# Moving GpSimd's elementwise work of the feed-forward part and the attention to VectorE and ScalarE

## The chip, the cores and the metric

One Trainium2 chip, one core of it. The core has TensorE (PE, matmuls; its weight loads are shown as PEld), VectorE (DVE), ScalarE (ACT), GpSimd (POOL) and SyncE (SP, which issues the transfers here). The metric is the device time of one execution in microseconds (us), the median of several runs.

## The reference

Three parts behind one another, in float32 (weights come as 64-bit numbers): attention with a window and a few always visible keys, a feed-forward part with a norm in front, and a part that turns the channels by an angle, mixes over tokens and ends in a gated channel product.

```python
batch, n_heads, seq, head_dim = (2, 8, 768, 64)      # d_model = 512
n_sink, window = (4, 128)
scores = np.where(is_sink | in_window, scale * q @ k.T, -1e9)
a = softmax(scores) @ v
# feed-forward
xn = (x - mu) / np.sqrt(var + 1e-06) * g_ln
x = x + np.maximum(xn @ w_ch1, 0.0) @ w_ch2            # 512 -> 2048 -> 512
# mixing
theta = x @ w_theta
yr = np.einsum('ts,bsd->btd', w_tok_r, x * np.cos(theta))
yi = np.einsum('ts,bsd->btd', w_tok_i, x * np.sin(theta))
u = x + yr + yi
return u + np.maximum(u @ w_ch, 0.0)
```

## The kernel before

The 1536 tokens are cut into six pieces of 256 tokens (two tiles of 128). For each piece the attention is computed head by head (8 heads), then the norm (`norm`), then the feed-forward part. The hidden width of 2048 is cut into 16 blocks; a *unit* `u` multiplies one block of both weight matrices: `first(u)` gives the hidden block `h`, `second(u)` adds its product to the accumulators. Two pieces run in the units at a time, and each pair of pieces joins eight units after the other, so there are 56 units. The order of TensorE's instructions is written out by hand (attention steps are put between the matmuls of the units by `advance`); that of the other engines is made by a scheduler that plays the program against its own model of durations. Each engine works off its queue in order. After the units comes the mixing part (`gate`, `mix`, `final`).

Precision: a float32 number is split into a high part, which TensorE takes as `fp32r`, and a low part, the difference; a product is then three matmuls (high x high, high x low, low x high). The high part is a copy on ScalarE, the low part a subtraction on another engine. The splits are these: `split_qk` (L234, queries and keys), `split_v` (L202 or L204 and L205, values, in float16), `split_w12` (L609 and L610, the feed-forward weights, once in each `first` and `second` from unit 8 on; `wh` and `wl` have three buffers each), L646 (the hidden block, whose input lies in PSUM), `split_w` (L684 and L685, weights of the mixing part).

The weights come as 64-bit numbers. `load64` makes float32 of them in four steps: L517 (VectorE) takes the sign, L518 (ScalarE) rescales the exponent word in place, L521 (GpSimd) or L524 (ScalarE) takes the last bits, L525 (VectorE) puts the words together. The 32 tiles of the feed-forward weights go by L521, those of the mixing part by L524. Four staging tiles take the transfers of the feed-forward weights; the next transfer into one is issued when L525 has freed it.

GpSimd's part of the work before: L610 up to unit 50 (VectorE does those of the last five units), L234 but for the first, L204 and L205 but for the first four tiles, L521, L629 (the low half of the first piece's normalized tokens), L574 (the norm's factor `gain` for pieces 2 to 5), L563 (a power), and in the mixing part L685 and L738.

Of the kernel before, what the change touches and what calls it, by code (L numbers as in the profile page):

```python
# [8 lines left out]
F32 = mybir.dt.float32  # L9
# [5 lines left out]
AF = mybir.ActivationFunctionType  # L15
# [56 lines left out]
class Net:  # L72
# [110 lines left out]
    def split_v(self, b, t):  # L183

        if (b, t) in self.v3:
            return
        nc, p = self.nc, self.att
        r = p["vr"].tile([128, DM], F32, tag="vr", name="vr")
        nc.sync.dma_start(out=r, in_=self.vt[b, t])
        eng = nc.vector if len(self.v3) < V_DVE else nc.gpsimd  # L190
        if t == NT:
            o = p["v"].tile([128, DM], F16, tag="vk", name="vk", bufs=1)
            nc.scalar.activation(o, r, AF.Copy, scale=VSC)
            r, lo, hi = r[64:96], o[64:96], o[64:96]
            self.v3[b, t] = o
        else:
            o = p["v"].tile([128, 2, DM], F16, tag="v", name="v")
            hi, lo = o[:, 0], o[:, 1]
            nc.scalar.activation(hi, r, AF.Copy, scale=VSC)
            self.v3[b, t] = hi, lo  # L200
        if eng is nc.vector:
            eng.scalar_tensor_tensor(out=lo, in0=r, scalar=VSC, in1=hi, op0=ALU.mult, op1=ALU.subtract)  # L202
        else:
            eng.tensor_scalar(out=r, in0=r, scalar1=VSC, scalar2=0.0, op0=ALU.mult, op1=ALU.add)  # L204
            eng.tensor_tensor(out=lo, in0=r, in1=hi, op=ALU.subtract)  # L205

    def range_v(self, b, t):

# [296 lines left out]
            yield  # L505


    def load64(self, src, stage, dst, tag, eng=None):

        nc = self.nc  # L510
        n = dst.shape[-1]
        raw = stage.tile([128, n, 2], I32, tag=tag, name="raw")
        nc.sync.dma_start(out=raw.rearrange("p n w -> p (n w)"), in_=src.bitcast(I32))
        hi, flat = raw[:, :, 1], raw.rearrange("p n w -> p (n w)")
        half = flat.bitcast(U16).rearrange("p (n w) -> p n w", w=4)
        parts = dst.bitcast(U16).rearrange("p (n w) -> p n w", w=2)
        nc.vector.tensor_scalar(out=parts[:, :, 1], in0=half[:, :, 3], scalar1=0x8000, scalar2=None, op0=ALU.bitwise_and)  # L517
        nc.scalar.activation(hi.bitcast(F32), hi.bitcast(F32), AF.Copy, scale=2.0 ** -112)  # L518

        if eng:  # L520
            eng.tensor_scalar(out=parts[:, :, 0], in0=half[:, :, 1], scalar1=2.0 ** -13, scalar2=2.0 ** -14 - 0.5,  # L521
                              op0=ALU.mult, op1=ALU.add)
        else:
            nc.scalar.activation(parts[:, :, 0], half[:, :, 1], AF.Copy, scale=2.0 ** -13, bias=2.0 ** -14 - 0.5)  # L524
        nc.vector.scalar_tensor_tensor(out=dst, in0=hi, scalar=3, in1=dst, op0=ALU.logical_shift_left,  # L525
                                       op1=ALU.bitwise_or)

# [7 lines left out]
    def load_w12(self, f):  # L535
        if f in self.w12f:
            return
        self.w12f[f] = []
        for e in range(2):
            t = self.wraw.tile([128, DM], I32, tag="w", name="w12")  # L540
            self.rawp.append(self.rawp.pop(0))
            self.load64(self.w12[f, e], self.rawp[-1][0], t, self.rawp[-1][1], self.nc.gpsimd)
            self.w12f[f].append(t.bitcast(F32))

    def stats(self, piece, half):
# [7 lines left out]
    def norm(self, piece):  # L553

        nc = self.nc
        mv = self.ln.tile([128, PIECE, 2], F32, tag="mv", name="mv")
        rs = self.ln.tile([128, PIECE], F32, tag="rs", name="rs")
        x, bn = self.x[piece], self.bn.pop(piece)
        xn = [self.ln.tile([128, DM], F32, tag="xn", name="xn", bufs=2) for _ in range(PIECE)]
        for i in range(PIECE):  # L560
            nc.vector.bn_aggr(out=mv[:, i], in_=bn[:, i])
        nc.scalar.activation(rs, mv[:, :, 1], AF.Copy, bias=1e-6)
        nc.gpsimd.tensor_tensor(out=rs, in0=rs, in1=self.mhalf, op=ALU.pow)  # L563
        if piece < DIRECT:
            for i, a in enumerate(xn):
                nc.vector.scalar_tensor_tensor(out=a, in0=x[:, i], scalar=mv[:, i, 0:1], in1=self.gain,
                                               op0=ALU.subtract, op1=ALU.mult)
            for i, a in enumerate(xn):
                nc.vector.tensor_scalar(out=a, in0=a, scalar1=rs[:, i:i + 1], scalar2=None, op0=ALU.mult)
        else:  # L570
            for i, a in enumerate(xn):
                nc.vector.tensor_scalar(out=a, in0=x[:, i], scalar1=mv[:, i, 0:1], scalar2=rs[:, i:i + 1],
                                        op0=ALU.subtract, op1=ALU.mult)
                nc.gpsimd.tensor_tensor(out=a, in0=a, in1=self.gain, op=ALU.mult)  # L574
        self.xnorm[piece] = xn

    def norm_T(self, piece):
# [23 lines left out]

        return piece % 2 if len(active(u)) > 1 else 0

    def split_w12(self, f, e, u=0):
        nc = self.nc
        r = self.w12f[f][e]
        hi = self.wsp.tile([128, DM], F32R, tag="wh", name="wh")
        lo = self.wsp.tile([128, DM], F32R, tag="wl", name="wl")
        nc.scalar.activation(hi, r, AF.Copy)  # L609
        (nc.vector if u >= UNITS - 5 else nc.gpsimd).tensor_tensor(out=lo, in0=r, in1=hi.bitcast(F32), op=ALU.subtract)  # L610
        return hi, lo

    def first(self, u):

        nc, part = self.nc, active(u)
        if u < WHOLE:
            h = self.hp.tile([128, PC], F32, tag="hh", name="hh")
            ps = self.ps_h.tile([128, 512], F32, tag="h", name="h")
            self.h[u] = h
            for k in range(KD):  # L620
                nc.tensor.matmul(ps[:, 0:PC], self.w12f[u][0][:, k * 128:(k + 1) * 128], self.x32[:, k],
                                 start=k == 0, stop=k == KD - 1)
            nc.scalar.activation(h, ps[:, 0:PC], AF.Relu)
            yield
            if u == WHOLE - 1:
                hi, lo = (x[:, :, 0] for x in self.xn)
                for k in range(KD):
                    nc.scalar.activation(hi[:, k], self.x32[:, k], AF.Copy)
                    nc.gpsimd.tensor_tensor(out=lo[:, k], in0=self.x32[:, k], in1=hi[:, k].bitcast(F32), op=ALU.subtract)  # L629
            return  # L630
        wh, wl = self.split_w12(u % NF, 0, u)
# [18 lines left out]
    def second(self, u):  # L650
# [2 lines left out]
        if u < WHOLE:  # L653
            prods = [(self.h.pop(u), self.w12f[u][1])]
        else:
            wh, wl = self.split_w12(u % NF, 1, u)
            hh, hl = self.h.pop(u)
            prods = [(hh, wh), (hh, wl), (hl, wh)]
        for piece in active(u):
# [131 lines left out]
    def run(self, general):  # L791
# [276 lines left out]
```

## Time and profile before

| | us |
|---|---|
| median of 3 runs | 630.4 |
| lowest and highest run | 625.32, 630.4 |
| profiled execution | 629.58 |
| its span, first to last instruction | 627.8 |

| engine | busy us | share of the span | instructions |
|---|---|---|---|
| PE | 570.5 | 91% | 3545 |
| DVE | 385.2 | 61% | 813 |
| ACT | 334.1 | 53% | 738 |
| POOL | 275.5 | 44% | 228 |

An instruction is told by its line and engine, by `output<-input` in the program's names and by its operands (partitions x elements, type); `x32` is their number. "Idle before" is the time the engine stood still in front of such instructions, with what ended it. A wait is written as `who <- for whom: total us, times, longest us`. In a table of stretches each engine has its busy us and, in brackets, its instructions; PEclk is the granted clock of TensorE as a share of 2.4 GHz.

### The profile page before, as it was taken

How to read it: one execution, taken by the hardware profiler on the slowest of the kernel's cores; microseconds unless marked ns; L12 is line 12 of the kernel's file. 1: busy time of each engine (PE TensorE's matmuls, PEld its weight loads, DVE VectorE, ACT ScalarE, POOL GpSimd, SP SyncE). 2: the span in 40 equal slices, each digit the busy share in tenths (PEclk: the TensorE clock that was granted, in tenths of full speed). 3: DMA queues.
4: the chain of work that ended last, by engine and by line, in shares of the span. 5: the costliest groups of instructions: out<-in, count | busy, mean ns of one | idle time of the engine just before them, and what ended most of it. 6: DMA issues, size and time to landing. Idle time of an engine off the chain costs nothing.

```text
span 627.8 us, 9676 instructions
## 1 busy us (share of the span) xinstructions
PE 570.5 (91%) x3545; PEld 470.6 (75%) x3545; DVE 385.2 (61%) x813; ACT 334.1 (53%) x738; POOL 275.5 (44%) x228
## 2 busy tenths in 40 slices
PE   4864779699999999999999969999999889999996
PEld 3753556466777776777788758888899789999996
DVE  5699999666455666737454331126898879754262
ACT  5674767376655655665545533346676666632120
POOL 4376684234673665556357634450334432201100
PEclk9999998799999999999999979999999999999998
DMA  6357756344503343232412220000323312011102
GB/s 255 116 197 250 251 197 206 77 105 83 119 18 80 82 98 65 65 64 45 69 60 93 99 78 0 2 0 1 101 70 119 115 66 69 1 34 34 36 27 81
DMA packets 54794, 55.39 MB, mean 88 GB/s; under 512 B 40016, under 2 KB 43088, under 8 KB 54736
## 3 DMA queue, kind: packets, MB, share of 16 engines
q1 hardware_dynamic: 54736, 54.67, 29.7%
q8 instruction: 30, 0.49, 0.3%
q14 instruction: 28, 0.23, 0.1%
HBM read 42.08 MB, written 3.15 MB: 72 GB/s over the span
## 4 chain that ended last, share of the span: by engine, by line
PE 53%; DVE 20%; ACT 7%; DMA 5%; issue 4%; POOL 3%; ACTq 0%; POOLq 0%; DVEq 0%; SPq 0%
PE acc L667 17%; PE h L641 16%; PE m L752 5%; PE f L783 5%; PE s L259 5%; DVE st L525 2%; DMA raw<-w 2%; DMA raw<-wtok 2%; DVE w L525 2%; PE pv L439 2%; PE th L711 2%; DVE w L517 2%; DVE st L517 1%; ACT raw L518 1%; ACT st L524 1%
## 5 line engine op out<-in xcount | busy, mean ns | idle before, releaser
L610 POOL TENSOR_TENSOR wl<-w,wh 128x512 fp32r<-128x512 f32 x86 | 113.6, 1323 | 116.7 <-ACT wh L609 87.5
L641 PE MATMUL h<-xT,wh 128*128 128x512 f32 (+1 forms) x384 | 94.7, 382 | 0.0
L609 ACT ACTIVATE wh<-w 128x512 fp32r<-128x512 f32 x96 | 60.1, 628 | 60.3 <-PE acc L667 39.0
L361 ACT ACTIVATE p<-p,st 128x272 f32<-128x272 f32 (+1 forms) x96 | 47.7, 497 | 59.4 <-DVE st L358 59.4
L641 PEld LDWEIGHTS h<-xT,wh 128*128 128x128 f32 x384 | 66.3, 188 | 15.4 <-issue 1.2
L667 PE MATMUL acc<-wh,hh 128*128 128x512 f32 x176 | 73.6, 418 | 0.0
L667 PE MATMUL acc<-wl,hh 128*128 128x512 f32 x176 | 69.7, 396 | 0.5 <-POOL wl L610 0.5
L667 PE MATMUL acc<-wh,hl 128*128 128x512 f32 x176 | 69.6, 395 | 0.0
L646 DVE SCALAR_TENSOR_TENSOR hl<-h,hh 128x512 fp32r<-128x512 f32 (+1 forms) x48 | 30.8, 641 | 52.8 <-ACT hh L645 52.8
L358 DVE CUSTOM_DVE_ANT_0 p<-s,mask 128x272 f32<-128x272 f32 (+1 forms) x96 | 39.0, 409 | 32.3 <-PE s L259 31.5
L518 ACT ACTIVATE raw<-raw 128x512 f32<-128x512 f32 (+1 forms) x52 | 37.8, 727 | 25.2 <-DVE w L517 16.3
L234 POOL TENSOR_TENSOR lo<-raw,hi 128x672 fp32r<-128x672 f32 (+1 forms) x23 | 36.9, 1604 | 31.8 <-ACT hi L233 31.6
L738 POOL TENSOR_TENSOR x<-xh,xl 128x512 f32<-128x512 f32 x12 | 19.3, 1609 | 67.7 <-DVE r L732 67.7
L641 PE MATMUL h<-xT,wl 128*128 128x512 f32 (+1 forms) x192 | 48.0, 372 | 0.0
L259 PE MATMUL s<-hi 64*128 64x272 f32 (+1 forms) x96 | 38.7, 409 | 10.2 <-ACT hi L233 6.9
L439 PEld LDWEIGHTS <-wt 128*128 128x128 f16 x576 | 23.4, 103 | 26.7 <-issue 12.3
L259 PEld LDWEIGHTS s<-hi 64*128 64x128 f32 x96 | 20.0, 212 | 27.9 <-issue 10.4
L439 PE MATMUL pv<-v,wt 128*128 128x64 f16 x528 | 27.7, 201 | 14.4 <-DVE x L456 8.3
L667 PEld LDWEIGHTS acc<-wh,hh 128*128 128x128 f32 x176 | 33.6, 191 | 9.3 <-issue 0.8
L385 DVE SCALAR_TENSOR_TENSOR w<-p,w 128x512 f16<-128x512 f32 (+2 forms) x40 | 35.2, 879 | 7.9 <-ACT w L384 7.5
L641 PEld LDWEIGHTS h<-xT,wl 128*128 128x128 f32 x192 | 34.4, 188 | 6.5
L667 PEld LDWEIGHTS acc<-wh,hl 128*128 128x128 f32 x176 | 33.5, 190 | 7.8 <-DVE hl L646 0.3
(290 smaller groups left out, 1544.6 us busy)
## 6 DMA issues: line engine op xcount, KB each, us to landing
raw<-w SPq DMA_DIRECT2D x32, 512.0 KB, 4.3
raw<-wtok SPq DMA_DIRECT2D x12, 768.0 KB, 4.2
raw<-qk SPq DMA_DIRECT2D x16, 336.0 KB, 3.1
vr<-vt SPq DMA_DIRECT2D x14, 256.0 KB, 3.0
out_dram<-o SPq DMA_DIRECT2D x24, 128.0 KB, 1.7
raw<-qk SPq DMA_DIRECT2D x8, 272.0 KB, 3.8
raw<-wth SPq DMA_DIRECT2D x4, 512.0 KB, 3.3
raw<-wch SPq DMA_DIRECT2D x4, 512.0 KB, 3.3
```

What stands on the lines that cost most here:

```text
L234: eng.tensor_tensor(out=lo, in0=r, in1=hi.bitcast(F32), op=ALU.subtract)
L259: self.nc.tensor.matmul(ps, q[:, c], k[:, k0:k0 + kn], start=j == 0, stop=j == 2)
L358: self.newest = [nc.vector.tensor_tensor_reduce(out=e, in0=ps[:, c0:WIN], in1=self.mask[min(t, 2)], scale=-0.125, scalar=3e38, op0=ALU.add ...
L361: nc.scalar.activation(e, e, AF.Exp, bias=st[:, 0, i:i + 1], scale=-1.0, accum_out=st[:, 1, i:i + 1])]
L385: nc.vector.scalar_tensor_tensor(out=o[1], in0=src, scalar=PSC, in1=o[0], op0=ALU.mult, op1=ALU.subtract)
L439: nc.tensor.matmul(pv[:, i * D:(i + 1) * D], a, m, start=j == 0, stop=j == len(prods) - 1)
L518: nc.scalar.activation(hi.bitcast(F32), hi.bitcast(F32), AF.Copy, scale=2.0 ** -112)
L609: nc.scalar.activation(hi, r, AF.Copy)
L610: (nc.vector if u >= UNITS - 5 else nc.gpsimd).tensor_tensor(out=lo, in0=r, in1=hi.bitcast(F32), op=ALU.subtract)
L641: nc.tensor.matmul(ps[:, 0:n], a[:, k * 128:(k + 1) * 128], x[:, k, c], start=m == 0, stop=m == 11)
L667: nc.tensor.matmul(ps, a[:, c], w, start=m == 0 and n == 0, stop=m == NF - 1 and n == len(prods) - 1)
L752: nc.tensor.matmul(ps, z[i][e][:, c * 128:(c + 1) * 128], w[:, t], start=s == 0 and m == 0 and c % 2 == 0, stop=s == NT - 1 and m == 5 and ...
```

## The change

Elementwise work of GpSimd goes to VectorE: the low parts of queries and keys (L234), of values (L204 and L205, two instructions, become the one of L202), of the feed-forward weights (L610) and of the first piece's tokens (L629). For pieces 2 to 5 the norm takes the form that pieces 0 and 1 have, two instructions of VectorE for each tile. The last bits of the feed-forward weights (L521) go to ScalarE, by the instruction of L524. On GpSimd stay the power of the norm (L563), the low parts of the mixing part's weights (L685) and the sum of L738, beside what is done once at the start.

```diff
@@ split_v
-        eng = nc.vector if len(self.v3) < V_DVE else nc.gpsimd
...
-        if eng is nc.vector:
-            eng.scalar_tensor_tensor(out=lo, in0=r, scalar=VSC, in1=hi, op0=ALU.mult, op1=ALU.subtract)
-        else:
-            eng.tensor_scalar(out=r, in0=r, scalar1=VSC, scalar2=0.0, op0=ALU.mult, op1=ALU.add)
-            eng.tensor_tensor(out=lo, in0=r, in1=hi, op=ALU.subtract)
+        nc.vector.scalar_tensor_tensor(out=lo, in0=r, scalar=VSC, in1=hi, op0=ALU.mult, op1=ALU.subtract)
@@ load64 (load_w12 no longer passes nc.gpsimd as eng)
-        if eng:
-            eng.tensor_scalar(out=parts[:, :, 0], in0=half[:, :, 1], scalar1=2.0 ** -13, scalar2=2.0 ** -14 - 0.5,
-                              op0=ALU.mult, op1=ALU.add)
-        else:
-            nc.scalar.activation(parts[:, :, 0], half[:, :, 1], AF.Copy, scale=2.0 ** -13, bias=2.0 ** -14 - 0.5)
+        nc.scalar.activation(parts[:, :, 0], half[:, :, 1], AF.Copy, scale=2.0 ** -13, bias=2.0 ** -14 - 0.5)
@@ norm
-        if piece < DIRECT:
...
-        else:
-            for i, a in enumerate(xn):
-                nc.vector.tensor_scalar(out=a, in0=x[:, i], scalar1=mv[:, i, 0:1], scalar2=rs[:, i:i + 1],
-                                        op0=ALU.subtract, op1=ALU.mult)
-                nc.gpsimd.tensor_tensor(out=a, in0=a, in1=self.gain, op=ALU.mult)
+        for i, a in enumerate(xn):
+            nc.vector.scalar_tensor_tensor(out=a, in0=x[:, i], scalar=mv[:, i, 0:1], in1=self.gain,
+                                           op0=ALU.subtract, op1=ALU.mult)
+        for i, a in enumerate(xn):
+            nc.vector.tensor_scalar(out=a, in0=a, scalar1=rs[:, i:i + 1], scalar2=None, op0=ALU.mult)
@@ split_w12
-        (nc.vector if u >= UNITS - 5 else nc.gpsimd).tensor_tensor(out=lo, in0=r, in1=hi.bitcast(F32), op=ALU.subtract)
+        nc.vector.tensor_tensor(out=lo, in0=r, in1=hi.bitcast(F32), op=ALU.subtract)
@@ first
-                    nc.gpsimd.tensor_tensor(out=lo[:, k], in0=self.x32[:, k], in1=hi[:, k].bitcast(F32), op=ALU.subtract)
+                    nc.vector.tensor_tensor(out=lo[:, k], in0=self.x32[:, k], in1=hi[:, k].bitcast(F32), op=ALU.subtract)
@@ run (the engine that attn_fast hands to split_qk)
-        side = attn(nc.gpsimd)
+        side = attn(nc.vector)
```

## Rows read from the trace of the kernel before

**Rows 1.** the profile page: span and number of instructions

```profile
span 627.8 us, 9676 instructions
```

**Rows 2.** Busy us by stretch (instructions); then granted clock, DMA share, GB/s

```profile
core 0: us, PE busy (x) PEld busy (x) DVE busy (x) ACT busy (x) POOL busy (x), PEclk, DMA share, GB/s
30.00:120.00 90.00, 64.24 (x358) 45.05 (x358) 84.25 (x176) 58.62 (x150) 57.02 (x53) 0.92 0.64 207
120.00:330.00 210.00, 205.29 (x1242) 153.69 (x1243) 124.13 (x329) 122.87 (x323) 111.65 (x88) 1.00 0.33 72
360.00:390.00 30.00, 25.10 (x104) 20.37 (x103) 6.98 (x10) 10.72 (x17) 13.14 (x10) 0.89 0.13 50
450.00:540.00 90.00, 85.74 (x621) 80.19 (x620) 77.18 (x101) 59.43 (x91) 33.76 (x20) 1.00 0.25 85
```

**Rows 3.** TensorE's waits, 30 to 125 us: total us, times, longest

```profile
PE tp L587 <- DVE xn L569: 10.8, 3, 8.2
PE pv L439 <- DVE x L456: 8.3, 3, 3.7
```

**Rows 4.** Timeline of VectorE: start us, us, instruction, [idle before <-releaser]

```profile
73.16 0.67 DVE L525 SCALAR_TENSOR_TENSOR w<-raw,w 128x512 int32<-128x512 int32 x1
73.75 0.45 DVE L517 TENSOR_SCALAR w<-raw 128x512 uint16<-128x512 uint16 x1
...
82.81 1.41 DVE L525 SCALAR_TENSOR_TENSOR w<-raw,w 128x512 int32<-128x512 int32 x1
84.14 1.02 DVE L517 TENSOR_SCALAR w<-raw 128x512 uint16<-128x512 uint16 x1
...
130.32 0.18 DVE L391 SCALAR_TENSOR_TENSOR w<-p,w 128x32 f16<-128x32 f32 x1
```

**Rows 5.** Timeline of GpSimd at the same places

```profile
74.28 1.13 POOL L521 TENSOR_SCALAR w<-raw 128x512 uint16<-128x512 uint16 x1 [0.99 <-DMA raw<-w]
...
82.39 1.28 POOL L610 TENSOR_TENSOR wl<-w,wh 128x512 fp32r<-128x512 f32 x1
83.75 2.04 POOL L521 TENSOR_SCALAR w<-raw 128x512 uint16<-128x512 uint16 x2
```

**Rows 6.** Groups by line, VectorE, 30 to 120 us: busy us, mean ns | idle before

```profile
L525 DVE SCALAR_TENSOR_TENSOR w<-raw,w 128x512 int32<-128x512 int32 x32 | 28.4, 894 | 0.8 <-POOL w L521 0.7
L517 DVE TENSOR_SCALAR w<-raw 128x512 uint16<-128x512 uint16 x32 | 28.3, 890 | 2.3 <-DMA raw<-w 2.3
```

**Rows 7.** Groups by line, GpSimd, 30 to 120 us

```profile
L521 POOL TENSOR_SCALAR w<-raw 128x512 uint16<-128x512 uint16 x31 | 29.2, 943 | 21.1 <-DMA raw<-w 19.9
L234 POOL TENSOR_TENSOR lo<-raw,hi 128x672 fp32r<-128x672 f32 x6 | 10.5, 1754 | 3.5 <-ACT hi L233 3.2
L205 POOL TENSOR_TENSOR v<-vr,v 128x512 f16<-128x512 f32 x3 | 4.1, 1360 | 0.2
```

**Rows 8.** Timeline of ScalarE at 341 us

```profile
340.87 0.80 ACT L524 ACTIVATE st<-raw 128x512 uint16<-128x512 uint16 x1 [1.78 <-DMA raw<-wth]
341.54 0.64 ACT L518 ACTIVATE raw<-raw 128x512 f32<-128x512 f32 x1
```

**Rows 9.** ScalarE's waits, 30 to 120 us

```profile
ACT raw L518 <- DVE w L517: 16.3, 14, 3.7
```

**Rows 10.** Groups by line, VectorE, 120 to 330 us

```profile
L385 DVE SCALAR_TENSOR_TENSOR w<-p,w 128x512 f16<-128x512 f32 x22 | 23.2, 1054 | 2.8 <-ACT w L384 2.7
L646 DVE SCALAR_TENSOR_TENSOR hl<-h,hh 128x512 fp32r<-128x512 f32 x26 | 17.7, 682 | 5.6 <-ACT hh L645 5.6
L391 DVE SCALAR_TENSOR_TENSOR w<-p,w 128x32 f16<-128x32 f32 x22 | 11.5, 522 | 0.0
```

**Rows 11.** Groups by line, GpSimd, 120 to 330 us

```profile
L610 POOL TENSOR_TENSOR wl<-w,wh 128x512 fp32r<-128x512 f32 x50 | 66.1, 1324 | 74.3 <-ACT wh L609 54.3 <-PE h L641 19.4 <-ACT w L384 0.3
```

**Rows 12.** Groups by line, VectorE, whole span: the ten L610 it already has

```profile
L610 DVE TENSOR_TENSOR wl<-w,wh 128x512 fp32r<-128x512 f32 x10 | 7.6, 766 | 3.6 <-ACT wh L609 3.6
```

**Rows 13.** TensorE's waits, 330 to 390 us

```profile
PE tp L587 <- DVE hl L646: 4.9, 1, 4.9
```

More of the change, by code (lines that the diff above doesn't have):

```diff
@@ L505, in attn_general, with load64 @@
             yield
-    def load64(self, src, stage, dst, tag, eng=None):
+    def load64(self, src, stage, dst, tag):
         nc = self.nc
@@ L541, in load_w12 @@
             self.rawp.append(self.rawp.pop(0))
-            self.load64(self.w12[f, e], self.rawp[-1][0], t, self.rawp[-1][1], self.nc.gpsimd)
+            self.load64(self.w12[f, e], self.rawp[-1][0], t, self.rawp[-1][1])
             self.w12f[f].append(t.bitcast(F32))
@@ L563, in norm @@
         nc.gpsimd.tensor_tensor(out=rs, in0=rs, in1=self.mhalf, op=ALU.pow)
-        if piece < DIRECT:
-            for i, a in enumerate(xn):
-                nc.vector.scalar_tensor_tensor(out=a, in0=x[:, i], scalar=mv[:, i, 0:1], in1=self.gain,
-                                               op0=ALU.subtract, op1=ALU.mult)
-            for i, a in enumerate(xn):
-                nc.vector.tensor_scalar(out=a, in0=a, scalar1=rs[:, i:i + 1], scalar2=None, op0=ALU.mult)
-        else:
-            for i, a in enumerate(xn):
-                nc.vector.tensor_scalar(out=a, in0=x[:, i], scalar1=mv[:, i, 0:1], scalar2=rs[:, i:i + 1],
-                                        op0=ALU.subtract, op1=ALU.mult)
-                nc.gpsimd.tensor_tensor(out=a, in0=a, in1=self.gain, op=ALU.mult)
+        for i, a in enumerate(xn):
[3 more added lines that the diff above has]
+            nc.vector.tensor_scalar(out=a, in0=a, scalar1=rs[:, i:i + 1], scalar2=None, op0=ALU.mult)
         self.xnorm[piece] = xn
@@ L602, in lane, with split_w12 @@
         return piece % 2 if len(active(u)) > 1 else 0
-    def split_w12(self, f, e, u=0):
+    def split_w12(self, f, e):
         nc = self.nc
@@ L628, in first @@
                     nc.scalar.activation(hi[:, k], self.x32[:, k], AF.Copy)
[L629 removed]
+                    nc.vector.tensor_tensor(out=lo[:, k], in0=self.x32[:, k], in1=hi[:, k].bitcast(F32), op=ALU.subtract)
             return
[L631 removed]
+        wh, wl = self.split_w12(u % NF, 0)
         n = len(part) * PC
@@ L655, in second @@
         else:
-            wh, wl = self.split_w12(u % NF, 1, u)
+            wh, wl = self.split_w12(u % NF, 1)
             hh, hl = self.h.pop(u)
```

2 lines of the change are left out of this document (removed).

## The prediction, made before the changed kernel was run

> **What bounds the kernel now.** The span is 627.8 us and the profiled execution took 629.6 us, so 1.8 us lie around the span; the median of the three timed runs is 630.4 us, 0.8 us above that execution. I sum against 629.6. [rows 1]
>
> I read the busy times by stretch first. Three things are to be seen in them. From 120 to 330 us TensorE is busy 205 of 210 us, and from 450 to 540 us 85.7 of 90: there the matmuls set the pace, and work on the other engines matters only when it makes TensorE wait. From 30 to 120 us TensorE works 64 of 90 us while VectorE works 84 of 90: this is the start, in which the attention of the first pieces and the conversion of the 32 weight tiles of the feed-forward part share the engines, and VectorE sets the pace. From 360 to 390 us TensorE loses 5 us and its granted clock falls to 0.89. [rows 2] The waits of TensorE say the same of the start: of 27 us of waits from 30 to 125 us (seven rows, of which two are shown) the two largest, 10.8 and 8.3 us, are for VectorE (the normalized tile, and a buffer that `x` frees). [rows 3]
>
> Then the timeline of VectorE beside that of GpSimd. Near 73 us GpSimd stands idle for 0.99 us and VectorE's two weight instructions take 0.67 us (L525) and 0.45 us (L517). Ten microseconds later GpSimd works without a gap and the same two take 1.41 and 1.02 us. [rows 4, 5] So an instruction of VectorE that has to run beside one of GpSimd can take twice its time. Not all do: L646, which reads one operand from PSUM, means 682 ns in a stretch where GpSimd is busy half of the time, while L385 (both tensors in SBUF) means 1054 ns and the small L391 522 ns. [rows 10] VectorE's 84 us are therefore partly GpSimd's.
>
> **The change, part by part.**
>
> *The start, VectorE (30 to 120 us).* With the 31 instructions of L521 and the others gone from GpSimd, L517 falls from 890 to about 450 ns and L525 from 894 to about 670 ns: 32 x 0.44 + 32 x 0.22 = 21 us off. [rows 4, 6] What comes on: six L234 (672 columns; 0.68 us for 512 columns scaled by width is 0.90 us, 5.4 us), four of L205, which become one instruction each (L202; 0.68 us, 2.7 us; the three L204 and their partner vanish), the three L610 that fall into this stretch (0.70 us, 2.1 us) and the four of half width at L629 (0.45 us, 1.8 us). That is 12 us. [rows 7, 10, 12] VectorE goes from 84.3 to 75 us of 90. If the durations did not shrink at all it would be 96.
>
> *The start, ScalarE.* L521 goes to ScalarE as the form that L524 has for the other weights. The trace has it: 0.80 us, and the next activation starts 0.67 us after it. [rows 8] 31 of them are 20.8 us by the pitch and 24.8 us by the duration. ScalarE goes from 58.6 to 79.4 or 83.4 of 90 us. [rows 2, 7] Its largest wait there is L518 for L517, 16.3 us, which shrinks with L517. [rows 9] So the busiest engine of the stretch changes: VectorE at 84.3 before, ScalarE at 79.4 after. If ScalarE is kept as densely busy as VectorE is now (84.25 of 90, 0.936), the stretch takes 79.4/0.936 = 84.8 us, or 89.1 us by the longer duration: -5.2 to -0.9. The far bounds are 79.4 us if ScalarE never waits (-10.6) and, if all its idle time but those 16.3 us stays, 79.4 + 15.1 = 94.5 us (+4.5). I take -4, since the instruction stands in a queue of others and the pitch counts.
>
> A rule of the Trainium skill speaks against this part: ScalarE: Activation LUTs, section Rules for kernel authors, wants add and multiply on VectorE, not on ScalarE. The row agrees that VectorE is quicker at it (L517 is a like instruction, 0.45 us against 0.80); by the rule the 31 would cost VectorE 14 us and fill it to 89 of 90, so the sum by the rule has no gain in this stretch, and by the rows it has the -4.
>
> *The clock at the start.* 0.92 over 90 us means some 14 us at 1.2 GHz, which followed TensorE's waits. [rows 2, 3] At most 7 us were lost by it; with waits somewhat shorter I take -1 (0 to -3).
>
> *The long middle (120 to 330 us).* VectorE gets 50 L610 (0.70 us, 35.0 us), 13 L234 (23 in all, less the six of the start and four before it; 0.90 us at most, 11.7 us), six L202 (4.1 us) and one instruction more for each of eight tiles in the norm (like L517, 0.45 us: 3.6 us): 54 us. It gets rid of 22 x (1054 - 685) ns at L385 and 22 x (522 - 180) ns at L391, 15.6 us, if those fall to what VectorE needs alone (180 ns for the small one is what it takes at 130 us, with GpSimd idle). [rows 4, 10, 11] From 124 it goes to 163 of 210 us, 78%. TensorE covers this as long as what it needs next is ready: the low halves of the weights have three buffers. The nearest row with a busier VectorE is 450 to 540 us: 77.2 of 90 us, 86%, and TensorE loses 4.7% there against 2.2% here. [rows 2] On a line from 59% to 86% busy, 78% costs 0.7 x 2.5% of 210 us, some 3.7 us more than now; VectorE's own chains get shorter too (L385 and L391). I take +3, with 0 and +20 as bounds (the upper one is the rival below).
>
> Queued behind the moved instruction: each L610 waits for ScalarE's `wh`, which waits for TensorE to free a buffer. On GpSimd these waits were 74.3 us long here and only other L610 and L234 stood behind them. [rows 11] On VectorE the score's L358, `hl` and the attention's weights stand behind, and TensorE waits for those.
>
> *330 to 390 us.* TensorE's wait of 4.9 us at 361 us is for `hl`, [rows 13] queued on VectorE behind weight conversions that wait for their transfer; the half clock after it (0.89 of 30 us, 6.6 us at half) costs up to 3.3 us more. [rows 2] Their staging tile is freed by GpSimd's L685, which then has a queue of its own and comes earlier, by up to one L610, 1.3 us, for each tile. [rows 11] I take -2, from -8.2 (all gone) to +3 (L610 put behind the same waits). The norm of pieces 2 to 5 gets shorter, but lies tens of microseconds ahead of its use: nothing.
>
> *The rest.* Before 30 us VectorE is little loaded; after 450 us nothing is moved, and L685 and L738 stay on GpSimd. Nothing, plus or minus 2. No DMA is added or moved; the waits for a staging buffer change only with L525 and L234.
>
> Sum: -4 - 1 + 3 - 2 = -4, so 629.6 - 4 = 625.6 us.
>
> **The rivals.**
>
> *A: VectorE's order makes TensorE wait (slower).* The place is the middle. VectorE has 210 - 163 = 47 us idle, and L610's waits were 74.3 us. It decides once more than some 20 us of these waits hold up others (then VectorE is as full as from 450 to 540 us). With half of them, 37 us, 200 of 210 us are filled and TensorE would lose about 12 us beyond now; the start's -5 and what the half clock after such stalls would cost, some 5 (a stall of 4.9 us cost up to 3.3), cancel: 629.6 + 12 = 642 us (634 to 650). For it: the 74 us. Against: the ten L610 that VectorE already has waited 3.6 us in all, 0.36 us each. [rows 12]
>
> *B: ScalarE takes VectorE's place and the start gains nothing.* ScalarE at 83 of 90 us with the exponentials queued behind L518 and the new instruction, both waiting for transfers: 0 to +4 at the start, 0 to +3 in the middle, the stall at 361 us as it was: 632 us (628 to 637). For it: 88 to 93% busy. Against: 16.3 us of its waits go.
>
> *C: VectorE's durations do not shrink, it simply gets fuller.* 96 us of work for 90: +6, so 636 us. Beside it stands a rule: Trainium skill, Perfetto Trace Analysis, Optimizing Scalar/DVE Operations: with VectorE saturated, moving work off it, even to GpSimd, may make sense, though the two share a port of SBUF. The first half would make this change a loss, the second half says why it need not be. Its second half is borne out by what the timelines show: durations halve where GpSimd is idle. [rows 4, 5]
>
> *D: the start gains more.* VectorE's waits fall by half (10) and the stall at 361 us goes with its clock (8): 629.6 - 18 + 3 = 615 us (608 to 618).
>
> **How the numbers follow.** About 1% is what a measurement of this kernel can tell from no change: against 630.4, below 624.1 or above 636.7. Forecast 0.42 (own range 618 to 630, of which 0.25 lies below 624.1), A 0.22, B 0.23, C 0.03, D 0.10. Faster: 0.25 + 0.10 = 0.35. Slower: 0.19 of A, 0.03 of B, 0.02 of C = 0.24. Within 1%: the rest, 0.41. The range 613 to 642 leaves out about half of A and a third of D.
>
> **What would show it.** Right: L517 near 450 ns, L525 near 670, L385 near 690, L391 near 180 over the whole part before 450 us; ScalarE, not VectorE, busiest from 30 to 120 us; that stretch's end (the first matmuls of L641) some 4 to 5 us earlier; TensorE as busy as now from there to 330 us; L732 and L725 after 450 us unchanged. Wrong: TensorE waiting for `wl` or `hl` of VectorE in the middle (A), waits for ScalarE's `p` or `wt` at the start (B).

## The result, and the profile after

The changed kernel took 623.1 us (median of 12 runs, 619.97 to 625.82), the kernel before 630.45 us beside it: a ratio of 0.9895, with a 95% interval of 0.9868 to 0.9921. That is 1.05% faster, just beyond the 1% that the prediction took as the bound of what can be told, and 2.5 us below the predicted 625.6 us, inside its range. The span fell from 627.8 us [rows 1] to 621.3 us. Lines have moved: L510, L511, L513 and L514 of the changed kernel are L517, L518, L524 and L525 of before, L593 is L610, L629 is L646, L570 is L587, L378 and L384 are L385 and L391. In the experiments that pass an engine to `load64` everything from L514 on stands four lines lower (the joining instruction is L518, the bits are L514).

The page: its span and its table of engines.

```profile
span 621.3 us, 9554 instructions
...
PE 571.8 (92%) x3545; PEld 472.2 (76%) x3545; DVE 421.3 (68%) x944; ACT 353.0 (57%) x770; POOL 61.5 (10%) x55
```

The stretches of [rows 2] again, in the changed kernel (columns as there).

```profile
30.00:120.00 90.00, 63.95 (x364) 44.63 (x364) 73.85 (x195) 77.07 (x183) 1.53 (x2) 0.94 0.63 204
120.00:330.00 210.00, 209.30 (x1254) 156.38 (x1253) 149.81 (x407) 124.73 (x324) 6.30 (x6) 0.99 0.35 74
360.00:390.00 30.00, 28.87 (x122) 23.83 (x123) 12.80 (x20) 10.28 (x17) 0.00 (x0) 0.94 0.08 27
450.00:540.00 90.00, 87.20 (x626) 82.50 (x625) 76.93 (x100) 56.67 (x88) 32.05 (x20) 0.96 0.23 77
```

From 30 to 120 us TensorE is no busier than before (63.95 against 64.24 us), although VectorE got 10 us lighter; ScalarE is now the busiest engine there. From 120 to 330 us TensorE leaves out 0.7 us where it left out 4.7.

VectorE's groups by line, from 30 to 120 us and from 120 to 330 us: they answer [rows 6] and [rows 10].

```profile
L514 DVE SCALAR_TENSOR_TENSOR w<-raw,w 128x512 int32<-128x512 int32 x32 | 21.8, 681 | 1.6 <-ACT raw L511 1.6
L510 DVE TENSOR_SCALAR w<-raw 128x512 uint16<-128x512 uint16 x32 | 14.3, 456 | 7.1 <-DMA raw<-w 7.0
```

From 120 to 330 us (L378 by shape, the largest of three):

```profile
L593 DVE TENSOR_TENSOR wl<-w,wh 128x512 fp32r<-128x512 f32 x52 | 36.2, 696 | 26.7 <-PE h L624 19.4 <-ACT wh L592 7.0 <-issue 0.2
...
L629 DVE SCALAR_TENSOR_TENSOR hl<-h,hh 128x512 fp32r<-128x512 f32 x27 | 18.5, 684 | 0.0
L378 DVE SCALAR_TENSOR_TENSOR w<-p,w 128x512 f16<-128x512 f32 x22 | 15.0, 682 | 1.0 <-ACT w L377 0.9
...
L384 DVE SCALAR_TENSOR_TENSOR w<-p,w 128x32 f16<-128x32 f32 x22 | 4.0, 183 | 0.0
```

With GpSimd nearly idle, each form runs at the duration that the prediction read off its clear places: 681, 456, 682 and 183 ns, where it had 894, 890, 1054 and 522. `hl`, whose input lies in PSUM, is the same as ever (684 against 682).

TensorE's waits from 30 to 125 us, the four largest: they answer [rows 3].

```profile
PE tp L570 <- DVE xn L557: 12.1, 2, 9.6
PE pv L432 <- DVE x L449: 5.0, 2, 2.6
PE wp L400 <- DVE wt L404: 3.9, 2, 2.0
PE h L604 <- DVE x L576: 2.8, 1, 2.8
```

**Where the time went.** TensorE issues the same 3545 instructions in the same order in both kernels, and, up to the mixing part, in all experiments. (A few neighbours change places near 430 us of the kernel before.) So the start of one and the same matmul in two traces tells how far one kernel is ahead there; I call the difference to before its shift. The table gives, for each kernel's one profile, the shift at a matmul that begins at 149.9 us before, what is added up to the one at 354.9 us, to the one at 379.9 us, and to the last one at 621.5 us (us; minus is ahead).

| kernel | at 150 | 150 to 355 | 355 to 380 | 380 to the end | ratio, 95% interval |
|---|---|---|---|---|---|
| changed kernel | -2.0 | -2.3 | -1.9 | +0.4 | 0.9895 [0.9868, 0.9921] |
| e1_bits_pool | -6.6 | -2.3 | -0.8 | 0.0 | 0.9824 [0.9788, 0.9859] |
| e3_bits_dve | -6.2 | -2.3 | -1.0 | +0.4 | 0.9848 [0.9811, 0.9885] |
| e11_only_bits | +7.6 | +1.9 | -0.4 | 0.0 | 1.0087 [1.0058, 1.0115] |
| e10_bits_wl_pool | -4.4 | -1.8 | -1.5 | 0.0 | 0.9873 [0.9838, 0.9908] |
| n1_only_norm | -0.5 | -2.1 | -1.8 | 0.0 | 0.9919 [0.9894, 0.9944] |
| n2_only_attn | -2.5 | -1.5 | -0.5 | 0.0 | 0.9917 [0.9884, 0.9950] |
| e2_wl_pool | -0.3 | -2.3 | -1.9 | 0.0 | 0.9911 [0.9883, 0.9940] |
| e4_wl_twice | +4.7 | +4.1 | +0.3 | +0.1 | 1.0104 [1.0064, 1.0144] |
| e5_mix_dve | -0.3 | -2.3 | -1.6 | -5.9 | 0.9791 [0.9754, 0.9829] |
| e6_sum_dve | -0.9 | -2.3 | -2.0 | -5.3 | 0.9773 [0.9727, 0.9819] |
| f1_bits_pool_sum_dve | -8.1 | -2.3 | -1.7 | -5.3 | 0.9736 [0.9700, 0.9772] |
| f2_bits_dve_sum_dve | -5.8 | -2.3 | -2.3 | -5.3 | 0.9746 [0.9719, 0.9773] |

The first column also shows what one profile is worth in the start: e5 and e6 differ from the changed kernel only in the mixing part, and yet stand at -0.3 and -0.9 there where it stands at -2.0. e1 and f1, and e3 and f2, also differ there alone and stand 1.5 and 0.4 us apart. Differences below some 2 us in that column are not told apart; the second column repeats to 0.1 us. Before 150 us a single profile scatters more: n1, whose changed instructions come first at 169 us, is 3.3 us ahead at the matmul that begins at 121 us before, and 0.5 us at 150. A row adds up a single profile and not the medians: the changed kernel's comes to -5.8 us, its medians differ by 7.3.

### The profile page after: what moved, and what is told of

Its sections match the earlier page's. It is cut to its first block, busy times and chain, and to the rows that moved or that the text cites. A ratio compares the mean times of both kernels' runs of the same rounds, so it can differ in the third digit from the quotient of the medians.

```text
span 621.3 us, 9554 instructions
## 1 busy us (share of the span) xinstructions
PE 571.8 (92%) x3545; PEld 472.2 (76%) x3545; DVE 421.3 (68%) x944; ACT 353.0 (57%) x770; POOL 61.5 (10%) x55
## 4 chain that ended last, share of the span: by engine, by line
PE 70%; DVE 12%; DMA 9%; ACT 5%; issue 2%; POOL 1%; SPq 0%; ACTq 0%; DVEq 0%; POOLq 0%
PE acc L650 19%; PE h L624 18%; PE m L735 11%; PE s L252 8%; PE f L766 5%; DMA raw<-w 5%; PE th L694 3%; PE pv L432 3%; DMA raw<-wtok 2%; DVE st L514 1%; DVE w L514 1%; ACT raw L511 1%; DMA raw<-wth 1%; ACT st L513 1%; PE wp L400 1%
## 5 line engine op out<-in xcount | busy, mean ns | idle before, releaser
L593 DVE TENSOR_TENSOR wl<-w,wh 128x512 fp32r<-128x512 f32 x96 | 69.2, 725 | 60.8 <-PE h L624 31.7
L511 ACT ACTIVATE raw<-raw 128x512 f32<-128x512 f32 (+1 forms) x52 | 37.1, 716 | 6.7 <-DVE st L510 6.3
L650 PEld LDWEIGHTS acc<-wl,hh 128*128 128x128 f32 x176 | 33.5, 190 | 6.0 <-DVE wl L593 0.4
L721 POOL TENSOR_TENSOR x<-xh,xl 128x512 f32<-128x512 f32 x12 | 19.3, 1605 | 130.6 <-DVE r L715 125.1
L552 POOL TENSOR_TENSOR rs<-rs,mhalf 128x2 f32<-128x2 f32 x6 | 5.2, 874 | 271.6 <-ACT rs L551 271.4
L252 PE MATMUL s<-lo,hi 64*128 64x272 f32 (+1 forms) x96 | 30.3, 320 | 0.7 <-DVE lo L227 0.7
```

The costliest lines, as they stand in the source:

```text
L252: self.nc.tensor.matmul(ps, q[:, c], k[:, k0:k0 + kn], start=j == 0, stop=j == 2)
L593: nc.vector.tensor_tensor(out=lo, in0=r, in1=hi.bitcast(F32), op=ALU.subtract)
L650: nc.tensor.matmul(ps, a[:, c], w, start=m == 0 and n == 0, stop=m == NF - 1 and n == len(prods) - 1)
L721: nc.gpsimd.tensor_tensor(out=self.xt(t), in0=xt[0].bitcast(F32), in1=xt[1].bitcast(F32), op=ALU.add)
```

## The experiments

### The last bits: ScalarE, GpSimd or VectorE

The question was which part of the change makes the start gain so little. In e1 the bits of the feed-forward weights go back to GpSimd, in e3 to VectorE, all else as in the changed kernel:

```diff
-            self.load64(self.w12[f, e], self.rawp[-1][0], t, self.rawp[-1][1])
+            self.load64(self.w12[f, e], self.rawp[-1][0], t, self.rawp[-1][1], self.nc.gpsimd)   # e1; e3: self.nc.vector
```

> The changed kernel with one part undone: the last bits of the 32 feed-forward weight tiles go back to GpSimd, all else as after the change. Theory 1 (an instruction of VectorE that runs beside one of GpSimd is held up by it, and the gain is that this ends): the sign and the joining of the words mean about 0.85 us again in the start instead of 0.46 and 0.68, VectorE has some 90 us of work for the 90 us from 30 to 120, and the time is 627 to 632 us. Theory 2 (ScalarE, at 77 of 90 us, is now what holds the start back): without its 32 instructions the start is quicker, 618 to 622 us.

> The changed kernel with the last bits of the 32 weight tiles on VectorE instead of ScalarE (0.45 us each instead of 0.78). Theory 1 alone says: VectorE goes from 74 to 88 of 90 us in the start and sets its pace, 624 to 628 us. Theory 2 (ScalarE holds the start back): ScalarE goes from 77 to some 55 of 90 us, the start is quicker and the time is 618 to 622 us. If transfers pace the start, neither: 622 to 624 us.

And e11 is the other way round: the kernel before, with only the bits moved to ScalarE.

```diff
-            self.load64(self.w12[f, e], self.rawp[-1][0], t, self.rawp[-1][1], self.nc.gpsimd)
+            self.load64(self.w12[f, e], self.rawp[-1][0], t, self.rawp[-1][1])
```

> The kernel before with one part of the change alone: the last bits of the feed-forward weights go from GpSimd to ScalarE, everything else stays on GpSimd. Theory 1: 29 us of GpSimd's work less in the start, so the sign and the joining fall to some 0.6 and 0.75 us and the start gains some 3 us: 626 to 628 us. Theory 2 (ScalarE's 32 more instructions cost what putting the bits back on GpSimd gave, 3.5 us): no gain or a loss, 630 to 634 us.

Measured: e1 619.4 us, e3 621.5 us, both ahead of the changed kernel by 4 to 5 us at 150 us, as theory 2 had it; e11 637.2 us, 0.9% slower than before and more than theory 2 had expected (630 to 634). By the whole table, the four kernels of the changed one's kind with the bits on ScalarE (changed, e2, e5, e6; e4, which adds work, aside) stand at -2.0, -0.3, -0.9 and -0.3 at 150 us; the three with them on GpSimd (e1, e10, f1) at -6.6, -4.4 and -8.1; the two with them on VectorE (e3, f2) at -6.2 and -5.8. Between kernels that differ in the bits (and in nothing else before 150 us) that is 4 to 8 us, so the move to ScalarE costs some 4 to 8 us of the start and is a loss by itself; the gain is in the other parts.

The stretch from 30 to 120 us, in e1, then e3, then e11 (three kernels, columns as in the stretches above).

```profile
30.00:120.00 90.00, 65.88 (x377) 45.72 (x378) 82.73 (x199) 59.52 (x153) 27.22 (x30) 0.94 0.66 205
```

```profile
30.00:120.00 90.00, 66.47 (x376) 46.47 (x377) 83.36 (x229) 59.91 (x152) 1.88 (x2) 0.94 0.64 205
```

```profile
30.00:120.00 90.00, 61.07 (x333) 42.36 (x331) 69.75 (x160) 72.95 (x169) 22.81 (x19) 0.92 0.61 197
```

The two kernels with the busiest VectorE (82.7 and 83.4 of 90 us) are the fast ones, and in e11 no engine is above 82% and the start is the slowest of all. Busy shares do not rank these kernels. The bits on ScalarE do change how long a tile of weights is on its way through the four steps, from the start of L517 to the end of L525 (L510 to L514 or L518 in the others): the mean over the 32 tiles, from VectorE's timeline, is 4.85 us in the changed kernel against 4.1 in e1 and 4.2 in e3, and 5.4 in e11 against 4.5 before, so 0.7 to 0.9 us longer each time. But the tiles do not come later for it: the last of the 32 is joined at 108.7 us in the changed kernel, 109.0 in e1 and 107.2 in e3, and among TensorE's waits from 30 to 125 us there is none for a weight tile in these three. (In e11 the last is joined 2.6 us later than before, and TensorE stands 7.6 us behind at 150 us.) The joining of the last tile, in the changed kernel and in e1:

```profile
108.06 0.69 DVE L514 SCALAR_TENSOR_TENSOR w<-raw,w 128x512 int32<-128x512 int32 x1
```

```profile
108.33 0.68 DVE L518 SCALAR_TENSOR_TENSOR w<-raw,w 128x512 int32<-128x512 int32 x1
```

What TensorE waits for there is the attention and the norm (`x`, `wt`, `xn` in the rows of the result). The attention's activations share ScalarE's queue with the rescaling and, in the changed kernel, with the bits, which GpSimd took beside it. And the new instruction stops that queue for transfers. ScalarE's largest wait from 30 to 125 us, first in the changed kernel, then in e1:

```profile
ACT w L513 <- DMA raw<-w: 6.9, 10, 1.7
```

```profile
ACT raw L511 <- DVE w L510: 12.8, 11, 3.2
```

ScalarE waits in both, in e1 even longer; but in the changed kernel 17.6 us more work (77.1 against 59.5) share the queue with those waits and with the exponentials. One such wait in the changed kernel: TensorE's two matmuls that give `pv`, then ScalarE with the bits and, behind them, the attention's copy of `pv`.

```profile
96.04 0.38 PE L413 MATMUL pv<-ident,p 128*16 128x128 f32 x2
```

```profile
98.09 0.79 ACT L513 ACTIVATE w<-raw 128x512 uint16<-128x512 uint16 x1 [1.67 <-DMA raw<-w]
98.75 0.72 ACT L416 ACTIVATE ws<-pv 16x256 f16<-16x256 f32 x2
```

The copy L416 could have begun at 96.4 us and began at 98.75. GpSimd can afford such waits, as its row in e1 from 30 to 120 us shows (65.5 us for transfers, with only the norm's power behind them):

```profile
L514 POOL TENSOR_SCALAR w<-raw 128x512 uint16<-128x512 uint16 x28 | 25.4, 909 | 65.5 <-DMA raw<-w 65.5
```

e3 has no such waits: there the bits stand on VectorE behind L510, which had waited for the same transfer. That the time is lost in ScalarE's queue, by the attention's steps behind the bits, fits these rows, but is argued from them: no run kept the instructions on ScalarE and took only the waits away.

Here a rule of the Trainium skill, ScalarE: Activation LUTs, section Rules for kernel authors (add and multiply on VectorE, not on ScalarE), was right and the row that the prediction set against it was read wrongly: e3 follows the rule at 621.5 us, the changed kernel does not at 623.1 us (the intervals of their ratios just overlap), and at 150 us they stand 4 us apart. The price by the rule was sized well (14.3 us of bits on VectorE for the 14 foretold), and VectorE, at 83.4 us of 90 and not the 89 feared, did not hold the start back.

### The low halves of the feed-forward weights

e2 puts L610 up to unit 50 back on GpSimd and leaves the rest of the change.

```diff
-        nc.vector.tensor_tensor(out=lo, in0=r, in1=hi.bitcast(F32), op=ALU.subtract)
+        (nc.vector if u >= UNITS - 5 else nc.gpsimd).tensor_tensor(out=lo, in0=r, in1=hi.bitcast(F32), op=ALU.subtract)
```

> The changed kernel with one part undone: the low parts of the feed-forward weights up to unit 50 go back to GpSimd. Theory 1: the attention's two instructions for the weights' low part mean about 1.05 and 0.5 us again in the middle, and what TensorE waited there before (some 2 us) and at the stall near 360 us (some 2 us) comes back: 625 to 628 us. Theory 3 (VectorE's fuller queue costs something in the middle, as rival A says): 619 to 622 us.

Measured: 625.3 us, ratio 0.9911; the interval overlaps that of the changed kernel (0.9895), so the largest single part of the change, 86 instructions, is worth 1 us by the ratios and nothing that is told apart, and in the table nothing from 150 to 355 us (-2.3 both). What it does to VectorE works both ways: with L610 on GpSimd VectorE has 135.2 us of work from 120 to 330 us instead of 149.8, but its own instructions are longer (L378 of all shapes 733 ns against 542).

e4 asks what that lengthening is worth by itself. VectorE keeps L610, and GpSimd computes the same again into a tile that nobody reads.

```diff
         nc.vector.tensor_tensor(out=lo, in0=r, in1=hi.bitcast(F32), op=ALU.subtract)
+        if u < UNITS - 5:
+            again = self.wsp.tile([128, DM], F32, tag="wa", name="wa", bufs=1)
+            nc.gpsimd.tensor_tensor(out=again, in0=r, in1=hi.bitcast(F32), op=ALU.subtract)
```

> The changed kernel with work added and none moved: GpSimd computes the low parts of the feed-forward weights up to unit 50 once more, into a tile that nobody reads, while VectorE computes the ones that are used. Order and dependencies of the other engines stay. Theory 1: VectorE's instructions with both tensors in SBUF are slowed again (the attention's two mean about 1.0 and 0.5 us, the weights' low part itself over 0.8 us), those with an operand in PSUM are not, and the time is 625 to 630 us. Theory 4 (the gain is that the low parts come sooner, 0.7 us after the high part instead of 1.3, or that the order is better): 622 to 624 us.

Measured: 637.1 us, 14 us above the changed kernel and far above the 625 to 630 that theory 1 gave. The stretch from 120 to 330 us in e4:

```profile
120.00:330.00 210.00, 201.76 (x1225) 149.60 (x1223) 180.57 (x406) 120.36 (x322) 73.30 (x53) 1.00 0.35 75
```

Its groups by line there, VectorE's and then GpSimd's copy:

```profile
L593 DVE TENSOR_TENSOR wl<-w,wh 128x512 fp32r<-128x512 f32 x49 | 57.8, 1182 | 13.7 <-PE h L627 8.0 <-ACT wh L592 5.6
...
L632 DVE SCALAR_TENSOR_TENSOR hl<-h,hh 128x512 fp32r<-128x512 f32 x24 | 16.3, 678 | 0.0
...
L596 POOL TENSOR_TENSOR wa<-w,wh 128x512 f32<-128x512 f32 x49 | 70.3, 1434 | 133.3 <-ACT wh L592 81.0 <-issue 29.0 <-ACT st L443 15.6
```

Work that nobody waits for makes L593 take 1182 instead of 696 ns, and leaves the instruction with a PSUM operand alone (678 against 684). VectorE rises from 149.8 to 180.6 of 210 us, and TensorE falls from 209.3 to 201.8. By the shifts, 6.4 of the 15.1 us that e4 stands behind the changed kernel at the end are lost from 150 to 355 us and 2.2 in the stall behind it; the other 6.7 us are there at 150 us already, although GpSimd does only four instructions (4.7 us) from 30 to 120 us. Scatter of some 2 us is in it; the rest of that part is not explained. TensorE's waits in the middle, the three largest, are all for VectorE, and ScalarE waited little for the copy, which reads `wh` and could have held its buffers:

```profile
PE s L252 <- DVE st L351: 3.7, 6, 1.0
PE tp L570 <- DVE xn L557: 2.5, 1, 2.5
PE tp L570 <- DVE hl L632: 1.9, 3, 0.7
```

```profile
ACT wh L592 <- POOL wa L596: 1.5, 1, 1.5
```

What is shown is the slowing of VectorE by GpSimd, and that it turned into time in e4, with VectorE at 86% of the stretch, and into none that is told apart in e2, with VectorE at 64%. Where between them it begins was not measured, and the busy share alone does not tell it: in e6, below, VectorE is as full in the mixing part and TensorE loses 0.4 us of 90.

### What is left when bits and low halves go back

e10 is the changed kernel with both edits above undone (e1 and e2 together): the attention's low parts, the first piece's L629 and the norm remain.

> The changed kernel with both large parts undone: the last bits and the feed-forward weights' low parts stay on GpSimd; what remains of the change are the attention's splits, the norm and the first piece's low half on VectorE. If the parts add (putting the low parts back cost some 2 us, putting the bits back gave some 4): 620 to 623 us. If the gain of the bits on GpSimd needs GpSimd to be otherwise idle (theory 1): 624 to 629 us.

Measured: 623.25 us, ratio 0.9873, no slower than the whole change. Two edits that move 118 of the change's instructions (86 and 32) bring nothing together that these runs can measure: the bits lose, and the low halves are worth 3 us beside e1 by the ratios, which is not told apart (0.9873 against 0.9824, with intervals that just overlap). n1 and n2 take the rest apart, each from the kernel before:

```diff
-DIRECT = 2
+DIRECT = 6                              # n1: the norm of pieces 2 to 5 on VectorE
```

```diff
-V_DVE = 4
+V_DVE = 99                              # n2: values on VectorE
-        side = attn(nc.gpsimd)
+        side = attn(nc.vector)          # n2: queries and keys on VectorE
```

> The kernel before with one part of the change alone: the norm of pieces 2 to 5 takes the two VectorE instructions of pieces 0 and 1, so GpSimd keeps only the power (L563) of it. Theory (in the middle the gain of the change is the wait of VectorE for L563 at 231 to 233 us, behind a stretch of GpSimd's queue): the shift of TensorE against before is 0 up to 230 us, then -1.5 to -2.5 us and stays: 628 to 629 us, ratio 0.996 to 0.998. Rival (the two us at 231 come from the attention's low parts no longer standing in GpSimd's queue): no shift at 231 us, 630 us, ratio 0.999 to 1.002.

> The kernel before with one part of the change alone: the low parts of queries, keys and values (L234, and L205 as one instruction of L202) on VectorE; weights, bits and norm as before. Theory (the moved attention splits give the gain of 4.4 us up to 121 us that the changed kernel has with bits and weights back on GpSimd): shift -4 to -5 at 121 us, nothing added after, 625 to 626 us, ratio 0.991 to 0.994; GpSimd in the start falls from 57 to about 44 of 90 us, VectorE's L517 and L525 from 890 to 750 to 830 ns. Rival (that gain needs the first piece's low half L629 on VectorE, or the order that comes of all of it): -1 or less at 121 us, 629 to 631 us, ratio 0.998 to 1.002.

Measured: 625.4 us (ratio 0.9919) and 624.9 us (0.9917). Each alone gives nearly what the whole change gives. For n1 my theory had one place right and missed another: about -1.4 us at the step of 231 to 238 us, just short of what was expected, but 1.8 us more from 355 to 380 us, which I had put down to L610 in GpSimd's queue. For n2 the shift at 121 us is -4.4, as expected, but n1's scatter there is 3.3, so it proves little; 2 us of it are gone by 150 us, and against the expectation 1.5 us are added behind it. L517 fell further than expected, to 569 ns, and L525 stayed at 894. The rival of n1 (that the 231 us step comes from the attention's parts) is neither right nor wrong: both edits take the same step.

That step is a queue on GpSimd. VectorE's timeline in the kernel before, 231 to 238 us:

```profile
231.23 0.08 DVE L358 DVE_READ_ACCUMULATOR2_ANT st<- 128x1 f32 x1
233.05 1.98 DVE L572 TENSOR_SCALAR xn<-x,mv,rs 128x512 f32<-128x512 f32 x2 [1.74 <-POOL rs L563]
...
235.21 1.52 DVE L385 SCALAR_TENSOR_TENSOR w<-p,w 128x512 f16<-128x512 f32 x1
236.65 1.25 DVE L391 SCALAR_TENSOR_TENSOR w<-p,w 128x32 f16<-128x32 f32 x1
```

GpSimd's there:

```profile
231.06 1.29 POOL L610 TENSOR_TENSOR wl<-w,wh 128x512 fp32r<-128x512 f32 x1 [2.45 <-ACT wh L609]
232.31 0.70 POOL L563 TENSOR_TENSOR rs<-rs,mhalf 128x2 f32<-128x2 f32 x1
...
234.65 3.20 POOL L574 TENSOR_TENSOR xn<-xn,gain 128x512 f32<-128x512 f32 x2 [0.36 <-DVE xn L572]
```

And TensorE's, with the wait that comes of it:

```profile
238.31 0.39 PE L259 MATMUL s<-hi 64*128 64x272 f32 x1 [1.51 <-DVE st L358]
```

L563 is 0.7 us long, but stands behind L610, which waits 2.45 us for its buffer; VectorE stands for 1.74 us, then has L385 and L391 at twice their length beside L574, and TensorE waits 1.51 us for the scores. In n1 the norm's first instruction does not need the power, so it fills the time (VectorE's timeline of n1):

```profile
230.15 2.44 DVE L566 SCALAR_TENSOR_TENSOR xn<-x,mv,gain 128x512 f32<-128x512 f32 x2
...
233.18 0.88 DVE L569 TENSOR_SCALAR xn<-xn,rs 128x512 f32<-128x512 f32 x2 [0.23 <-POOL rs L563]
```

In n2 the power starts at 228.89 us, with no L204, L205 and L234 in GpSimd's queue in the 7 us ahead of it, and VectorE's wait is 0.82 us.

### The mixing part

The prediction left L685 and L738 out, since the change does. GpSimd's 32 us there lengthen VectorE's instructions as they did before (L708, which was L725, still 942 ns), so two more runs move them: e6 only the sum L738 (L721 of the changed kernel), e5 also the low halves L685 (L668).

```diff
-        nc.gpsimd.tensor_tensor(out=self.xt(t), in0=xt[0].bitcast(F32), in1=xt[1].bitcast(F32), op=ALU.add)
+        nc.vector.tensor_tensor(out=self.xt(t), in0=xt[0].bitcast(F32), in1=xt[1].bitcast(F32), op=ALU.add)
-        nc.gpsimd.tensor_tensor(out=lo, in0=r, in1=hi.bitcast(F32), op=ALU.subtract)   # e5 alone
+        nc.vector.tensor_tensor(out=lo, in0=r, in1=hi.bitcast(F32), op=ALU.subtract)
```

The first of the two texts on what was expected speaks of e5 as "the kernel before it".

> As the kernel before it in this call, but only the sum at the end of the gate goes to VectorE (12 instructions of 1.6 us on GpSimd, 0.69 on VectorE); the weights' low parts stay on GpSimd. Theory 1: 8 us on and about half of the hold-ups off: 621 to 624 us. Rival (more work in a full stretch): 624 to 627 us.

> The changed kernel taken further: in the mixing part too, the low parts of the weights and the sum at the end of the gate go from GpSimd to VectorE. Theory 1: VectorE's instructions there (now up to 1.06 us) fall to 0.69 and 0.43, 13 us off and some 25 us on in the stretch in which VectorE is busy 77 of 90 us; TensorE's waits for GpSimd there (2.3 us) go, others may come: 620 to 626 us. Rival (VectorE becomes the bound there): 626 to 632 us.

Measured: e6 616.3 us (0.9773), e5 619.2 us (0.9791): with its interval the second edit adds nothing. Both are faster than expected, e6 by 5 us: the expectation reckoned with VectorE's durations and not with the wait that went. TensorE's waits from 450 us on tell why e6 gains. The changed kernel's waits there:

```profile
PE m L735 <- POOL tok41l L668: 2.1, 1, 2.1
PE m L735 <- ACT tok41h L667: 0.5, 1, 0.5
PE m L735 <- POOL tok31l L668: 0.2, 1, 0.2
```

Two short stretches of it, in which the wait for `tok41l` lies:

```profile
488.80:495.60 6.80, 5.05 (x30) 4.10 (x28) 4.95 (x7) 4.46 (x8) 2.99 (x2) 1.00 0.36 115
495.60:502.40 6.80, 5.92 (x27) 5.92 (x28) 4.94 (x7) 3.66 (x5) 2.25 (x2) 0.50 0.20 69
```

In e6 the same two stretches:

```profile
488.80:495.60 6.80, 6.80 (x48) 6.22 (x47) 5.88 (x8) 5.31 (x8) 1.85 (x1) 1.00 0.38 117
495.60:502.40 6.80, 6.80 (x53) 6.54 (x53) 5.73 (x9) 4.42 (x8) 1.86 (x1) 1.00 0.27 83
```

And the line of e6 that was 942 ns, from 450 to 540 us:

```profile
L708 DVE TENSOR_SCALAR r<-r 128x512 f32<-128x512 f32 x8 | 4.9, 614 | 0.2
```

L668 (`tok41l`) stands behind L721 in GpSimd's queue, which waited 4.73 us for VectorE and took 1.61; with the sum on VectorE it comes in time, the wait of 2.1 us goes, and so does the stretch at half clock (0.50, that is 1.2 GHz) that follows it in the changed kernel. VectorE takes the sum almost without cost to its total: 78.0 of 90 us against 76.9.

The half clock is not what the gain hangs on. The kernel before has the full clock there [rows 2], and instead a wait for `tok51h` beside those of the changed kernel:

```profile
PE m L752 <- POOL tok41l L685: 2.1, 1, 2.1
PE m L752 <- ACT tok51h L684: 1.5, 1, 1.5
```

From 380 us to the end the two take the same time (+0.4 us in the table), with 4.3 us of waits in the one and 2.8 us of waits and 6.8 us at half clock in the other. In e6 0.4 us of waits are left and no half clock there.

The last two runs put the two findings together, with the bits on GpSimd (f1) or on VectorE (f2) and the sum on VectorE.

> The changed kernel with two edits together: the last bits of the feed-forward weights back on GpSimd (619.4 us alone) and the sum of the mixing part, L738 of before, on VectorE too (616.3 us alone). If both gains add, since one lies before 125 us and the other after 500 us: 0.9824 x 0.9773 / 0.9895 = 0.970 of before, some 612 us; busiest TensorE in both stretches (66 of 90 us from 30 to 120 us, 89.6 of 90 from 450 to 540 us). Rival (the earlier start is given back before the mixing part, whose start another thing sets, such as transfers): no better than 616 us, ratio 0.976 or more.

> The changed kernel with the last bits of the feed-forward weights on VectorE (621.5 us alone) and the sum of the mixing part on VectorE too (616.3 us alone): GpSimd keeps only the power of the norm and the low parts of the mixing weights. If both gains add: 0.9848 x 0.9773 / 0.9895 = 0.973 of before, some 613 to 614 us, 1 to 2 us behind the kernel that has the bits on GpSimd. Rival (VectorE, with 83 of 90 us in the start, gives back what GpSimd would have hidden): 616 us or more.

Measured: 613.8 us (0.9736) and 614.1 us (0.9746). The gains nearly add, as expected: 0.970 lies at the edge of f1's interval, and 0.973 within f2's. f1 and f2 are not told apart. Both beat the changed kernel by about 1.5% and the kernel before by about 2.6%.

## Why the prediction came out, point by point

The time was right, in part by luck: of the four terms of its sum the start and the middle were wrong, and their errors cancel (3 us too much gain in the one, 4.5 us too little in the other).

**Durations: right.** L517 456 ns for 450, L525 681 for 670, L385 682 for 690, L391 183 for 180, and L610 696 for 700. VectorE in the start 73.9 us for 75, ScalarE 77.1 for 79.4. GpSimd's share of VectorE's time was what the timelines [rows 4, 5] said, and rival C is out.

**The start, -5 with the clock: wrong in its reason.** Measured -2.0 at 150 us, and two more kernels with the same start, e5 and e6, say -0.3 and -0.9; the first matmul of L641 came 0.9 us earlier, not 4 to 5. The step that failed is "the busiest engine of the stretch changes", with the time worked out from ScalarE's busy share. VectorE's 84 of 90 us [rows 2] were taken for the pace of the start, but at 150 us e3 is 4 us ahead of the changed kernel with VectorE at 83.4, and e11 7.6 us behind the kernel before with VectorE at 69.8. What TensorE waits for in the start is the attention and the norm, whose steps go back and forth between VectorE and ScalarE, and instructions added to ScalarE's queue delay them; the first half of this is in the rows, the second fits them. With GpSimd cleared of the attention and the first piece's low half the start stands at -4.4 to -8.1 (e10, e1, f1), and the bits on ScalarE take some 4 to 8 us back. Rival B came nearest in the start (nothing gained, with the attention queued behind the bits); its 632 us did not come, since its other terms, the middle and the stall, went the other way.

**The middle, +3: wrong in sign.** From 150 to 330 us the shift goes from -2.0 to -3.5, so -1.5. VectorE got to 149.8 us, not 163: the shorter shapes of L385 shrank too (128x256 from 785 to 416 ns), and the busy time counts the overlap of instructions that follow each other once, while my sum added their whole durations (the groups of the stretch sum to 172 us after, 140 before). Of the line through 59% and 86% busy the upper point was taken from the mixing part, where L685 and L738 make TensorE wait, so its 4.7% were not VectorE's fullness: e6 has VectorE at 87% in that stretch and loses 0.4%, while e4 has 86% in the middle and loses 3.9%. And a gain was missed: the wait for the power L563 at 231 us, which was in the trace (1.74 us) and stood in no row of mine. Rival A did not come: L593 waited 26.7 us on VectorE, not 74.3 or half of it, and TensorE waited 0.6 us in the whole stretch.

**330 to 390 us, -2: right in size (-2.7), partly for other reasons.** The wait for `hl` went from 4.9 [rows 13] to 3.8 us, and the clock from 0.89 to 0.94 over the 30 us. But n1, which keeps L610 and L685 on GpSimd, has 1.8 us of it too, with a wait of 3.9 us; the earlier L685 is not needed for it. What moves that wait by 1 us in n1 was not settled.

**The rest, 0 within 2: right** (+0.4 from 380 us to the end). e6 shows that the mixing part has its own 5 us to gain, which the change does not touch.

## What to carry to other kernels

An engine that is busy for 94% of a stretch need not set its pace: before pricing a move by busy time, ask what the bound engine waits for, and what of that stands behind the moved instruction in its new queue. An instruction that waits for a transfer is best put where nothing urgent stands behind it, or behind another that has waited for the same transfer; this fits e1 and e3, and is not shown by a run of its own. In these runs VectorE's work took up to twice its time beside GpSimd's; this became time in e4 and not in e2, and what GpSimd cost at 231 us and in the mixing part was its queue, an instruction behind the long wait of another, so look there first.

## What was not expected of the hardware

GpSimd's copy in e4 slowed both sides: VectorE's 128x512 subtraction of two SBUF tensors went from 696 to 1182 ns, and GpSimd's own took 1434 ns in the mean and 1268 at the least; the VectorE instruction with a PSUM operand kept its time (684 and 678 ns). A rule of the Trainium skill, Perfetto Trace Analysis, section Optimizing Scalar/DVE Operations, says that the two share a read port of SBUF, so that moving work between them might not help. The trace agrees with the sharing: each of the two took longer beside the other.

At two of the places where the granted clock fell in the changed kernel it followed a wait of TensorE. One is the mixing part's, above, where it took the place of a wait that the kernel before has (`tok51h`). At the other, after the wait of 2.52 us that ends at 118.9 us, the granted clock was 0.72 from 120 to 126 us, and the second of two equal groups of four transposes took 1.06 us where the first took 0.66, as both these rows of TensorE show.

```profile
118.92 0.66 PE L570 MATMUL tp<-ident,xn 128*128 128x128 f32 x4 [2.52 <-DVE xn L557]
...
122.15 1.06 PE L570 MATMUL tp<-ident,xn 128*128 128x128 f32 x4
```

In e1 the wait before the same transposes is 0.44 us, the clock from 116 to 122 us is 1.00, and the second group takes 0.60 us. From the first group to 125 us e1's lead over the changed kernel goes from 2.9 to 4.5 us.
